# Moving the load of x from ScalarE's queue into SyncE's, between the two parts of wq

## The chip, the cores and the metric

The kernel runs on one core of a Trainium2 chip. The metric is the device time of one execution in microseconds. TensorE (PE), VectorE (DVE), ScalarE (ACT) and GpSimd (POOL) compute; here SyncE (SP) only issues DMA transfers, and ACT issues one.

## The reference, cut to what matters

One decode step of a transformer block for four sequences (B = 4): layer norm, attention over the last 4096 positions of a key and value cache, an output projection with a residual, then a second layer norm and a gated MLP with a residual.

```python
# x: [4, 1, 576]; caches: [4, 16, 16384, 128]; wq: [576, 4096]; wo: [4096, 576]
def attention(x, k_cache, v_cache, wq, wo):
    q = (x @ wq).reshape(4, 1, 32, 128)              # 32 query heads, 16 key/value heads
    k, v = k_cache[:, :, -4096:], v_cache[:, :, -4096:]   # each used by 2 query heads
    p = softmax(q . k * 128 ** -0.5)
    return (p . v).reshape(4, 1, 4096) @ wo

def mlp(x, W_gate, W_up, W_down):                    # [576, 4608] twice, [4608, 576]
    gate = x @ W_gate
    return ((gate * (gate > 0)) * (x @ W_up)) @ W_down

h  = x + attention(layernorm(x), ...)
h2 = h + mlp(layernorm(h), ...)
```

All tensors are bfloat16. About 160 MB are read in one execution, 134 MB of them the window of the two caches; x itself is 4.5 KB.

## The kernel before

The program of each engine is written out by hand, in a function of its own: `prog_sync`, `prog_act`, `prog_dve`, `prog_pool`, `prog_pe`. A small class `Sched` records a name for every operation and turns each name in a list of dependencies into a wait on a semaphore, ahead of the operation. So an engine works strictly in the order of its function, and an operation that waits holds up all behind it on that engine.

**Transfers.** SP works through one list, `transfers`, in order (`prog_sync`, L265). An entry has a name, a semaphore, what must be free before, and the DMA. The buffer `pool` holds four slots of 4 MB. `add` works out from the overlaps of offsets which consumer must be done before a slot is written again. The order is:

- wq4: rows 512 to 575 of wq, 512 KB, as 128 pieces of 4 KB (L234)
- wq0: rows 0 to 511, 4 MB, four consecutive rows for each partition (L236)
- K and V by turns, 32 transfers of 4 MB, each four heads of one sequence (L238 to L242)
- wo, W_gate, W_up, W_down (L243 to L256), and at last the store of the output (L268)

The first four entries (wq4, wq0 and the first two K) wait for nothing. The first V needs the place of wq0, so it waits for the end of the projection of q (QMM).

**x.** The only transfer that SP doesn't issue is x: it is the first line of `prog_act` (L303) and goes to `x_bf`, four partitions of 1152 bytes. It has two readers: the first layer norm, and the residual late in the kernel (L443).

**What follows x.** DVE takes the moments of x first (`moments`, L374 and L376), then builds constants from an identity matrix that POOL makes: sel, par, mask, mask8 (L384 to L390). Then it takes the reciprocal and writes `xn_bf` (`rows_norm`, L379 and L380). ACT, after x's DMA, waits for the moments, takes the root (L304), and then builds dup and col (L306, L308). PE turns `xn_bf` (L476), and multiplies it first with wq4 and then with wq0 (the loop over c = 4, 0, 1, 2, 3 in `prog_pe`). ACT copies the queries out (L320), and DVE turns them after its first transpose of a K tile (L402, L428).

**The main loop.** For each of the 16 K transfers DVE transposes four quarters (L402), PE multiplies them with the queries, DVE, POOL and ACT make the softmax, and PE multiplies with V one step later. The last stages are the output projection, the second norm and the MLP, whose W_down comes in six pieces that get smaller.

Of the kernel before, what the change touches and what calls it, by code (L numbers as in the profile page):

```python
# [102 lines left out]
def bass_sequential_preLN__sliding_block_cached__glu_gated_reglu__decode_kernel(  # L103
# [12 lines left out]
    with ExitStack() as es:  # L116
        cnt = [0]

        def sb(name, shape, dt):
            return es.enter_context(nc.sbuf_tensor(name, shape, dt))  # L120
# [10 lines left out]
        x_bf = sb("x_bf", [B, D], BF16)  # L131
# [64 lines left out]
        S = Sched()  # L196
# [3 lines left out]
        transfers = []  # L200
        at = {}

        def add(name, key, off, n, consumer, make):

            free = []
            for u in list(users):
                if u[0] < off + n and off < u[1]:
                    if u[2] not in free:
                        free.append(u[2])
                    if off <= u[0] and u[1] <= off + n:  # L210
                        users.remove(u)
            users.append((off, off + n, consumer))
            at[name] = off
            transfers.append((name, key, free, lambda e: make(e, pool[:, off:off + n])))
# [12 lines left out]
        def add_V(i):  # L227
# [5 lines left out]

        add(("wq", 4), "wq4", 2 * QUAD + 4 * HQ, HQ // 2, "QMM",  # L234
            lambda e, o: e.dma_start(out=o, in_=A_wq[512:576, :].rearrange("r (u n) -> (r u) n", u=2)))
        add(("wq", 0), "wq0", 2 * QUAD, 4 * HQ, "QMM",  # L236
            lambda e, o: e.dma_start(out=o, in_=A_wq[0:512, :].rearrange("(p u) n -> p (u n)", u=4)))
        for m in range(NQUAD + VLEAD):  # L238
# [14 lines left out]
        for k, (f0, f1) in enumerate(WD):  # L253
            transfers.append((("wd", k), f"wd{k}", ["ATTN"],
                              lambda e, f0=f0, f1=f1: e.dma_start(
                                  out=pool[:, f0 * D:f1 * D], in_=B_W_down.rearrange("(p j) n -> p (j n)", j=JJ)[:, f0 * D:f1 * D])))  # L256
# [4 lines left out]
        def land(name):  # L261
            return ("L",) + (name if isinstance(name, tuple) else (name,))
# [37 lines left out]

        def prog_act(S):
            a = "scalar"
            S.dma(a, lambda e: e.dma_start(out=x_bf[:, :], in_=A_x.rearrange("b s d -> (b s) d")), "x", name=land("x"))  # L303
            S.op(a, lambda e: e.activation(out=st1[:, 14:15], in_=st1[:, 13:14], func=ACT.Sqrt, bias=eps_c[0:B, 0:1], scale=1.0),  # L304
                 deps=["D_VAR", "EPS"], name="A_STD")
            S.op(a, lambda e: e.copy(out=dup[:, :].rearrange("p (r u) -> p r u", u=2),  # L306
                                     in_=bass.AP(tensor=ident_b, offset=0, ap=[[128, 64], [1, 64], [0, 2]])), deps=["IDB"], name="DUP")
            S.op(a, lambda e: e.copy(out=col[:, :].rearrange("p (a s) -> p a s", s=NS),  # L308
                                     in_=bass.AP(tensor=ident_b, offset=0, ap=[[128, NS], [0, 128], [1, NS]])), name="COL")
# [3 lines left out]
                                           in_=bass.AP(tensor=ident_b, offset=0, ap=[[128, NS], [0, 16], [1, NS], [0, 2]]),  # L313
# [5 lines left out]
            for k in range(2):  # L319
                S.op(a, lambda e, k=k: e.copy(out=q_bf[:, k, :].rearrange("p (x e k) -> p x e k", e=2, k=32),  # L320
                                              in_=pb[QB[k]].rearrange("p (x k e) -> p x e k", e=2, k=32)), deps=["QMM"], name=f"QBF{k}")
            S.op(a, lambda e: e.copy(out=qrep[:, :, :].rearrange("p x (g y) -> p x g y", g=4),  # L322
                                     in_=sc.ap().rearrange("p (g r) -> p g r", g=4)[:, :, 0:128].rearrange("p g (x y) -> p x g y", x=4)),
# [17 lines left out]
            for i in range(NQUAD):  # L341
# [3 lines left out]
                if i >= 2:  # L345
                    deps.append(("TRP", i - 2))
                S.op(a, lambda e, i=i: e.activation(  # L347
                    out=Pb[:, (i % 2) * 1024:(i % 2 + 1) * 1024], in_=sc[:, (i % 2) * 1024:(i % 2 + 1) * 1024], func=ACT.Exp,
                    scale=SCALE, bias=bias[:, i % 2:i % 2 + 1], accum_out=rs1[:, i:i + 1]),
                    deps=deps, name=("EXP", i))  # L350
                if i + 2 < NQUAD:
                    qzero(i + 2)
            S.op(a, lambda e: e.copy(out=bass.AP(tensor=spread, offset=0, ap=[[16 * H, H], [4 * H + 1, 4], [4, H]]),
                                     in_=bass.AP(tensor=ident_b, offset=0, ap=[[128, H], [0, 4], [1, H]])),
# [102 lines left out]
        def prog_pe(S):  # L457
# [127 lines left out]
            for k, (f0, f1) in enumerate(WD):  # L585
                deps = [land(("wd", k))]
                for f in range(f0, f1):
                    if f % (JJ // 2) == 0:
                        deps = deps + [("HHT", f // (JJ // 2))]
                    for u in range(2):  # L590
# [3 lines left out]
                        deps = []  # L594

        progs = [("gpsimd", prog_pool), ("sync", prog_sync), ("scalar", prog_act), ("vector", prog_dve), ("tensor", prog_pe)]
        S.begin(False)
        for _, p in progs:
# [32 lines left out]
```

## Time and profile before

| | |
|---|---|
| median of 3 runs | 377.9 us (377.59 to 378.06) |
| profiled execution | 378.37 us, its span 377.0 us |
| busy share of the span | PE 77%, DVE 59%, ACT 14%, POOL 3% |
| read from memory | 159.58 MB, 423 GB/s over the span |
| DMA queue 1 (issued by SP) | 6488 packets, 159.59 MB |
| DMA queue 10 (issued by ACT) | 8 packets, 4.5 KB of data |
| DMA queues 8 and 14 (loads of instructions) | 11 packets, 0.15 MB |

The span is from the first to the last instruction of the profiled execution. An engine's busy share is an average over all stages. A line of the timeline has the start and the duration in microseconds, the engine (SPq and ACTq are the sequencers that issue DMAs), the line of the kernel, the operation with output and input, and in brackets how long the engine had been idle before and what ended that. DMA transfers are split over up to 16 DMA engines; each has its own ring for each queue. The trace also keeps a record of each packet (queue, start, duration, size) and of each landing on a semaphore, without the number of the DMA engine.

### The profile page before, as it was taken

How to read it: one execution, taken by the hardware profiler on the slowest of the kernel's cores; microseconds unless marked ns; L12 is line 12 of the kernel's file. 1: busy time of each engine (PE TensorE's matmuls, PEld its weight loads, DVE VectorE, ACT ScalarE, POOL GpSimd, SP SyncE). 2: the span in 40 equal slices, each digit the busy share in tenths (PEclk: the TensorE clock that was granted, in tenths of full speed). 3: DMA queues.
4: the chain of work that ended last, by engine and by line, in shares of the span. 5: the costliest groups of instructions: out<-in, count | busy, mean ns of one | idle time of the engine just before them, and what ended most of it. 6: DMA issues, size and time to landing. Idle time of an engine off the chain costs nothing.

```text
span 377.0 us, 2565 instructions
## 1 busy us (share of the span) xinstructions
PE 291.9 (77%) x1384; PEld 67.9 (18%) x740; DVE 222.5 (59%) x169; ACT 53.1 (14%) x138; POOL 12.1 (3%) x34
## 2 busy tenths in 40 slices
PE   1408299969996999499939996799689967977675
PEld 0001012212221222022202221122112211222213
DVE  3037577696859494859476856775676658221230
ACT  3003402010220012001200220021002010101020
POOL 6000000000000000000000000000000000000000
PEclk9999879998998799989998998999869995996989
DMA  8999999999999999999999999999999999999995
GB/s 334 431 445 441 403 438 440 441 418 424 437 441 428 414 441 436 435 410 441 441 426 421 435 445 428 431 422 441 431 435 415 441 435 428 447 428 416 418 417 245
DMA packets 6507, 159.74 MB, mean 424 GB/s; under 512 B 729, under 2 KB 865, under 8 KB 1633
## 3 DMA queue, kind: packets, MB, share of 16 engines
q1 hardware_dynamic: 6488, 159.59, 98.7%
q8 instruction: 8, 0.13, 0.1%
q14 instruction: 3, 0.02, 0.0%
q10 hardware_dynamic: 8, 0.00, 0.0%
HBM read 159.58 MB, written 0.00 MB: 423 GB/s over the span
## 4 chain that ended last, share of the span: by engine, by line
DMA 53%; DVE 28%; PE 15%; ACT 2%; issue 1%; SPq 1%; POOL 0%; DVEq 0%
DMA pool<-in_A_k_cache_dram 48%; DVE kT L402 19%; PE sc L464 5%; PE sc L466 5%; DMA pool<-in_B_W_down_dram 5%; DVE acc L421 4%; DVE own_sb L418 2%; PE val L464 2%; PE val L466 2%; DVE probT L415 1%; DVE rmx L405 1%; ACT P L347 1%; DVE o_bf L440 0%; ACT L347 0%; ACT qz L336 0%
## 5 line engine op out<-in xcount | busy, mean ns | idle before, releaser
L402 DVE STREAM_TRANSPOSE kT<-pool 128x2048 f32<-128x2048 f32 x64 | 142.9, 2279 | 34.9 <-DMA pool<-in_A_k_cache_dram 33.9
L464 PE MATMUL sc<-kT,qz 128*128 128x512 bf16 x240 | 104.4, 435 | 28.7 <-DVE kT L402 28.7
L466 PE MATMUL sc<-kT,qz 128*128 128x512 bf16 x256 | 110.4, 431 | 18.3 <-DVE kT L402 16.2
L464 PE MATMUL val<-pool,probT 128*64 128x512 bf16 (+2 forms) x328 | 102.4, 360 | 4.6 <-DMA pool<-in_B_W_down_dram 4.6
L466 PE MATMUL val<-pool,probT 128*64 128x512 bf16 x256 | 96.2, 379 | 0.0
L464 PEld LDWEIGHTS sc<-kT,qz 128*128 128x128 bf16 x256 | 26.9, 105 | 154.8 <-issue 76.3
L464 PEld LDWEIGHTS val<-pool,probT 128*64 128x64 bf16 (+1 forms) x328 | 31.4, 104 | 88.0 <-issue 78.1
L405 DVE TENSOR_REDUCE rmx<-sc 128x1 f32<-128x1024 f32 x16 | 19.6, 1225 | 42.4 <-PE sc L466 42.4
L342 ACT ACTIVATE pmax<-mask,rmx 128x8 f32<-128x8 f32 x16 | 4.8, 301 | 241.3 <-DVE rmx L405 241.3
L415 DVE STREAM_TRANSPOSE probT<-P 128x1024 bf16<-128x1024 bf16 x16 | 19.9, 1245 | 20.7 <-ACT P L347 20.7
L347 ACT ACTIVATE P<-sc,bias 128x1024 bf16<-128x1024 f32 x16 | 17.8, 1113 | 13.3 <-DVE bias L410 13.3
L336 ACT COPY qz<-qrep 32x128 bf16<-32x128 bf16 x64 | 18.8, 294 | 0.6
L294 POOL PARTITION_ALL_REDUCE bcm<-pmax x16 | 5.9, 367 | 312.8 <-ACT pmax L342 312.8
L421 DVE TENSOR_REDUCE acc<-own_sb 128x128 f32<-128x1024 f32 x8 | 15.2, 1895 | 0.3
L418 DVE TENSOR_TENSOR own_sb<-val,mask 128x1024 f32<-128x1024 f32 x8 | 9.5, 1193 | 8.3 <-PE val L466 8.3
L464 PE MATMUL sc<-pool,oX 128*4 128x288 bf16 x32 | 10.2, 345 | 0.4 <-ACT oX L356 0.4
L408 DVE SCALAR_TENSOR_TENSOR t<-bcm,mask 128x8 f32<-128x8 f32 x16 | 2.7, 167 | 13.3 <-POOL bcm L294 13.3
L466 PE MATMUL sc<-pool,oX 128*4 128x288 bf16 x32 | 10.2, 343 | 0.0
L464 PE MATMUL sc<-qT,sel 32*128 32x128 bf16 x4 | 0.3, 284 | 9.8 <-DVE qT L428 9.8
L443 DVE TENSOR_TENSOR h_row<-sc,x_bf 4x576 f32<-4x576 f32 x1 | 0.7, 745 | 11.9 <-PE sc L466 11.9
L464 PE MATMUL sc<-col,foe 4*128 4x512 bf16 x16 | 6.4, 399 | 0.7 <-ACT qrep L322 0.7
L464 PE MATMUL val<-pool,xnT 128*32 128x512 bf16 x16 | 2.6, 628 | 5.0 <-DMA pool<-in_A_wq_dram 5.0
(98 smaller groups left out, 74.4 us busy)
## 6 DMA issues: line engine op xcount, KB each, us to landing
pool<-in_A_k_cache_dram SPq DMA_DIRECT2D x16, 4096.0 KB, 26.9
pool<-in_A_v_cache_dram SPq DMA_DIRECT2D x16, 4096.0 KB, 26.8
pool<-in_A_wo_dram SPq DMA_DIRECT2D x1, 4608.0 KB, 18.3
pool<-in_B_W_gate_dram SPq DMA_DIRECT2D x1, 4608.0 KB, 17.8
pool<-in_B_W_up_dram SPq DMA_DIRECT2D x1, 4608.0 KB, 24.0
pool<-in_A_wq_dram SPq DMA_DIRECT2D x1, 4096.0 KB, 13.6
pool<-in_B_W_down_dram SPq DMA_DIRECT2D x1, 2016.0 KB, 13.7
pool<-in_B_W_down_dram SPq DMA_DIRECT2D x1, 1296.0 KB, 16.4
```

Of the source, the lines that this page charges most:

```text
L294: S.op(g, lambda e, i=i: e.partition_all_reduce(bcm[:, i % 2, :], pmax[:, i % 2, :], 128, bass_isa.ReduceOp.max), deps=deps, name=("PAR", i))
L336: S.op(a, lambda e, src=src, dst=dst: e.copy(out=dst, in_=src), deps=deps, name=("QZ", i) if g == 3 else None, signal=g == 3)
L342: S.op(a, lambda e, i=i: e.activation(out=pmax[:, i % 2, :], in_=mask[:, 1, :], func=ACT.Identity, bias=rmx[:, i % 2:i % 2 + 1], scale=1.0 ...
L347: S.op(a, lambda e, i=i: e.activation(out=Pb[:, (i % 2) * 1024:(i % 2 + 1) * 1024], in_=sc[:, (i % 2) * 1024:(i % 2 + 1) * 1024], func=ACT ...
L402: S.op(v, lambda e: e.transpose(out=dst, in_=src), deps=deps, name=("TR", f))
L405: S.op(v, lambda e: e.tensor_reduce(out=rmx[:, i % 2:i % 2 + 1], in_=sc[:, (i % 2) * 1024:(i % 2 + 1) * 1024], axis=AX.X, op=ALU.max), dep ...
L408: S.op(v, lambda e: e.scalar_tensor_tensor(out=t8[:, :], in0=bcm[:, i % 2, :], scalar=-SCALE, in1=mask[:, 0, :], op0=ALU.mult, op1=ALU.mul ...
L415: S.op(v, lambda e: e.transpose(out=pT[i % NPT], in_=Pb[:, (i % 2) * 1024:(i % 2 + 1) * 1024]), deps=[("EXP", i)] + ([("PV", i - NPT)] if ...
L418: S.op(v, lambda e: e.tensor_tensor(out=own_sb[:, :].rearrange("p (x d) -> p x d", d=DH), in0=val[:, :].rearrange("p (x d) -> p x d", d=DH ...
L421: S.op(v, lambda e: e.tensor_reduce(out=acc[:, w % 2, :], in_=own_sb[:, :].rearrange("p (x d) -> p d x", d=DH), axis=AX.X, op=ALU.add), de ...
L464: return e.matmul(o, lhsT=l, rhs=r, start=start, stop=stop, skip_group_check=skip)
L466: return e.add_instruction(mybir.InstMatmult(name=nc.get_next_instruction_name(), start_tensor_calc=start, stop_tensor_calc=stop, bass_ski ...
```

## The change

x becomes an entry of SP's list, after wq4 and before wq0, with the same DMA and the same semaphore, and no wait. The line in ACT's program goes. Both readers still wait for the name of x's landing.

```diff
         add(("wq", 4), "wq4", 2 * QUAD + 4 * HQ, HQ // 2, "QMM",
             lambda e, o: e.dma_start(out=o, in_=A_wq[512:576, :].rearrange("r (u n) -> (r u) n", u=2)))
+        transfers.append((("x",), "x", [], lambda e: e.dma_start(out=x_bf[:, :], in_=A_x.rearrange("b s d -> (b s) d"))))
         add(("wq", 0), "wq0", 2 * QUAD, 4 * HQ, "QMM",
             lambda e, o: e.dma_start(out=o, in_=A_wq[0:512, :].rearrange("(p u) n -> p (u n)", u=4)))
...
         def prog_act(S):
             a = "scalar"
-            S.dma(a, lambda e: e.dma_start(out=x_bf[:, :], in_=A_x.rearrange("b s d -> (b s) d")), "x", name=land("x"))
             S.op(a, lambda e: e.activation(out=st1[:, 14:15], in_=st1[:, 13:14], func=ACT.Sqrt, bias=eps_c[0:B, 0:1], scale=1.0),
                  deps=["D_VAR", "EPS"], name="A_STD")
```

## The prediction

> **What bounds the kernel now.** I read the page first: the slices, the queues and the chain.
>
> ```profile
> span 377.0 us, 2565 instructions
> ...
> DMA  8999999999999999999999999999999999999995
> ...
> q1 hardware_dynamic: 6488, 159.59, 98.7%
> ...
> q10 hardware_dynamic: 8, 0.00, 0.0%
> ...
> DMA 53%; DVE 28%; PE 15%; ACT 2%; issue 1%; SPq 1%; POOL 0%; DVEq 0%
> ```
>
> The DMA row is full in every slice but the first and the last. Queue 1 (SP's) holds 98.7% of the engines' time; queue 10 is ACT's, whose only transfer is x: 8 packets, four rows and four semaphore writes. The chain of waits names DVE and PE often, but they wait for K tiles, and SP issues each K or V about 27 us before it lands while one passes in 9.7: the queue always holds two more. So the time is: start of SP's stream, plus the stream, plus what follows the last piece of W_down. The packet records of the trace agree: each of the 16 engines takes one 32 KB packet after another, 1.21 us each, with a gap only where an instruction load cuts in.
>
> Then the timeline of the first 28 us, where the edit lies.
>
> ```profile
> 0.72 0.55 ACTq L303 DMA_DIRECT2D x_bf<-in_A_x_dram  x1
> ...
> 0.72 0.41 SPq L235 DMA_DIRECT2D pool<-in_A_wq_dram  x1
> ...
> 1.18 0.41 SPq L237 DMA_DIRECT2D pool<-in_A_wq_dram  x1
> ...
> 1.64 1.32 SPq L225 DMA_DIRECT2D pool<-in_A_k_cache_dram  x2
> 2.16 0.81 DVE L374 BATCH_NORM_STATS2 st<-x_bf 4x6 f32<-4x288 bf16 x2 [2.16 <-DMA x_bf<-in_A_x_dram]
> ...
> 5.02 1.01 DVE L384 TENSOR_REDUCE sel<-ident_b 128x128 bf16<-128x512 bf16 x1 [1.81 <-POOL ident_b L278]
> ...
> 6.79 0.42 DVE L380 TENSOR_SCALAR xn_bf<-x_bf,st 4x576 bf16<-4x576 bf16 x1
> ...
> 14.81 0.62 PE L464 MATMUL val<-pool,xnT 128*32 128x512 bf16 x4 [5.04 <-DMA pool<-in_A_wq_dram]
> ...
> 18.48 0.54 SPq L230 DMA_DIRECT2D pool<-in_A_v_cache_dram  x1
> ...
> 24.69 2.31 DVE L402 STREAM_TRANSPOSE kT<-pool 128x2048 f32<-128x2048 f32 x1 [17.48 <-DMA pool<-in_A_k_cache_dram]
> ```
>
> x has two kinds of room. DVE has its moments long before it can build sel: it idles 1.81 us for the identity. And PE, done with the odd rows of wq (wq4) at 9.77, idles 5.04 us (9.77 is 14.81 less these) until the rest (wq0) lands. Nothing in this stage limits but the stream itself.
>
> **The change, part by part.** Durations are the profiled execution's: 378.37 us, its span 377.0 and 1.37 around it; it lies 0.47 above the median of 377.9, so I add my sum to the median.
>
> *SP's queue.* x's issue comes ahead of wq0's, K0's and K1's. No row has that issue on SP. ACT's issue of the same transfer took 0.55; SP's store of the output, also four rows of 1152 bytes, took 0.35:
>
> ```profile
> 375.71 0.35 SPq L268 DMA_DIRECT2D out_dram<-out_sb  x1
> ```
>
> I take 0.40, near that row (same queue, same four rows), and keep 0.35 and 0.55. With the 0.06 between issues, wq0 is issued 0.41 to 0.61 later, at 1.59 to 1.79 instead of 1.18. The cover is wq4 in the rings: its first packets started 1.03 (first engine) to 1.36 us (last) after its issue, so wq0's packets stand ready at 2.62 to 3.15, while the engines end wq4 between 3.26 and 3.66. Even the last engine to be supplied against the first to run dry leaves 0.11 us: no gap, 0.00. With that cover gone the end would come 0.41 to 0.61 later. K0 and K1 have more: their first packets are wanted at 13.2 and 22.9. V0, the next issue, waits for the projection's end at 18.48 in either case.
>
> *The rings.* x's packets took 0.05 to 0.12 us on four engines, and will do so there again, behind wq4 instead of ahead of it: 0.00. What a ring adds between two transfers is 6 ns: wq4's semaphore write at 3.262, wq0's first packet at 3.268, though wq4 landed from 3.60 on; so the engines do not wait for a landing before the next transfer. Without a second queue beside it wq4 may start up to 0.10 us sooner (x's first packet at 1.65, wq4's at 1.75): between -0.10 and 0; I take 0, because the first packets of wq4 took up to 0.83 us against 0.16 later, on more engines than x has rows: it is the start itself that is slow there.
>
> *x's landing.* Before, 1.42 us from issue to landing, at 2.14. After, it is issued at 1.18: at the earliest it lands at 2.60; at the latest behind all of wq4, 4.06 plus a packet of 0.12, say 4.2. I take 4.1, as rings keep their order. DVE's moments then run to 5.15 (0.81, 0.20 and gaps), and sel, par, mask, mask8, the reciprocal and xn, queued behind them, move by 0.15. ACT's root, the first in its queue, moves from 3.24 to 5.2; dup and col behind it start at 5.5 instead of 5.02, and PE wants dup only at 7.94. PE's five turns and the eight matmuls of wq4 follow 0.15 later, ending at 9.92. The 5.04 us of waiting for wq0 become 4.89: on the path 0.00. That cover ends only if x lands after about 9; and then the queries, ready at 19.55, have 7.4 us more before DVE reads them at 26.93.
>
> *ACT's queue.* Its issue of 0.55 goes. The table load behind it may start before 1.36; ACT then waits for x: 0.00.
>
> Sum: 0 (bounds -0.10 and 0 with the issue hidden, +0.61 with its cover gone), so 377.9 us.
>
> The Trainium skill has a rule against this change: "DMA: Bandwidth & Descriptors", section "Issuing engines are not separate DMA queues", says that transfers of all issuing engines run interleaved on the same 16 DMA engines and that a second issuing engine saves only sequencer time. By that the move gains nothing and gives back one issue, which would be a sum above zero instead of zero if it showed. The trace agrees on the shared engines (x on ring 10 and wq4 on ring 1 start within 0.1 us of each other); the rival below called the issue shown is what the rule would make of the time.
>
> **The rivals.** About 0.2% (0.76 us) is what a measurement of this kernel can tell from no change.
>
> *The issue shown.* If wq0's descriptors take longer after a four-row transfer than after nothing, the rings run dry at 3.3 to 3.7 and every later packet is late by that: 0.41 to 0.61, 378.4 us. It decides from an issue delay of 0.72 on (3.26 less 1.18 and 1.36); it passes 0.2% only from 1.5 us. Against it: three issues on SP in a row stand 0.46 apart.
>
> *The four slow packets gone (faster).* The packet records show one oddity: four packets of wq0, started at 11.99 to 12.12 on four engines, took 1.97 to 2.34 us instead of 1.21, with no other packet beside them. These engines stay late to the end, and one of them, hit again by an 8 KB instruction load at 100.7, is the last in each later landing: the final piece of W_down lands from 372.46 to 374.83, the next-to-last engine at 374.25. Were this a trace of the second queue (x too used four engines), it would go, and the end would come 0.58 sooner, with the earlier start 0.68: 377.2 us. Against it: it comes 10 us after x, and by the order of first packets these are not the engines that started beside x's packets.
>
> *An instruction load on the slowest engine (slower).* Queue 8 moves eight loads of 16 KB. Each holds up one engine's ring by about 1.0 us and stretches its next packet by 0.5. The landings show that each hit another engine (nine of sixteen end 1.5 to 1.8 us behind the first: these eight, and one of the four slow ones that an 8 KB load hit at 78.4) and that none hit the last, which is 2.38 behind. SP's program gets an instruction longer and ACT's shorter; if that moves one load to the slowest engine, every later landing is 1.5 us later: 379.4 us. It decides as soon as one of eight does so. Against it: these look like PE's instructions (2124 of 2565 on the page), and PE's program is untouched; for it: nothing in the trace shows what ties a load to an engine.
>
> That the change does not do what it says is hard to see: both readers of x wait for the name that the new transfer carries.
>
> **How the numbers follow.** No change (everything hidden): 0.58, 377.9 us, own range 377.5 to 378.3, which is the spread of the three runs with the sum's bounds. Four slow packets gone: 0.15. Instruction load: 0.15. Issue shown: 0.12. Faster by over 0.2%: half of the second (0.68 lies just inside 0.76) 0.08, and 0.05 for scatter in the first: 0.13. Slower: 0.15, a third of the last (0.04) and 0.04 of scatter: 0.23. Within 0.2%: 0.64. The range takes in the gone packets (377.2, less 0.1 of scatter) and the shown issue (378.5 at its dearest, plus 0.3); it leaves out the instruction load: 377.1 to 378.8.
>
> **What would show it.** Right: the issues in the order wq4, x, wq0 at about 0.72, 1.18 and 1.6; DVE's first wait for x near 4.1; PE's wait for wq0 near 4.9, ended at 14.8; K0's first transpose at 24.7 as before; the last landing near 374.8; queue 10 gone. A first transpose at 25.1 or later with wq0's landing moved alike means the issue shown; wrong on x would be PE's matmuls on the odd rows starting after 10 us. If the first transpose stands and the end moves, it is the lag of single DMA engines. The forecast is wrong if the median leaves 377.1 to 378.7.

## The result, and the profile after

The changed kernel is slower: 380.14 us (median of 6 runs, 379.56 to 381.0) against 378.01 for the kernel before, a ratio of 1.0059 with a 95% interval of 1.0044 to 1.0074. That is 2.13 us. A second set of 12 runs gave 379.34, ratio 1.0034 (1.0020 to 1.0048). The forecast was no change, 377.1 to 378.8 (378.7 in its last line).

The page of the profiled execution (380.75 us, span 379.4): span, queues, and the chain of waits by engine.

```profile
span 379.4 us, 2581 instructions
...
q1 hardware_dynamic: 6496, 159.59, 98.2%
...
DMA 48%; DVE 32%; PE 15%; ACT 3%; issue 1%; SPq 1%; POOL 0%; DVEq 0%
```

Queue 10 is gone, queue 1 has x's eight packets more, and its share has gone down: the same bytes, with idle time between. The timeline of the first 27 us says where.

```profile
0.72 0.39 SPq L235 DMA_DIRECT2D pool<-in_A_wq_dram  x1
...
1.17 0.36 SPq L236 DMA_DIRECT2D x_bf<-in_A_x_dram  x1
1.58 0.34 SPq L238 DMA_DIRECT2D pool<-in_A_wq_dram  x1
...
4.22 0.81 DVE L374 BATCH_NORM_STATS2 st<-x_bf 4x6 f32<-4x288 bf16 x2 [4.22 <-DMA x_bf<-in_A_x_dram]
...
6.91 0.42 DVE L380 TENSOR_SCALAR xn_bf<-x_bf,st 4x576 bf16<-4x576 bf16 x1
...
17.19 0.62 PE L464 MATMUL val<-pool,xnT 128*32 128x512 bf16 x4 [7.30 <-DMA pool<-in_A_wq_dram]
...
26.87 2.31 DVE L402 STREAM_TRANSPOSE kT<-pool 128x2048 f32<-128x2048 f32 x1 [19.55 <-DMA pool<-in_A_k_cache_dram]
```

Down to xn_bf all is as worked out. But wq0 lands at 17.15 instead of 14.77, PE waits 7.30 us for it instead of 5.04, and K0's first transpose starts at 26.87 instead of 24.69. The final piece of W_down lands at 377.22 instead of 374.83. So 2.38 us were lost before wq0 had landed, and 2.39 is what is missing at the end. In between the difference varies a little (K0's first transpose is 2.18 later), but none of it is won back by the end.

The packet records show the loss itself. In the kernel before, each of the 16 rings started its first 32 KB packet of wq0 within 0.04 us of its end of wq4, at 3.27 to 3.66. In the changed kernel eleven do so (3.45 to 3.73). The other five, which had ended wq4, or x behind it, between 3.42 and 3.53, start at 4.43, 5.02, 5.44, 5.44 and 5.49, and these packets then take 2.10 to 2.57 us instead of 1.21. Chained by their times, the records also say where x was: three of the five late rings carried no packet of x, and two of the four rings that carried one went on at once. At 5.88 to 6.30 one packet of each other ring is slow too (1.60 to 2.00).

Four theories were on the table: **A**, wq0's issue comes too late, and some rings run dry; **B**, the four-row transfer of x in SP's rings holds them up, whatever the time; **C**, taking x from ACT's queue costs by itself; and, from the prediction, that single slow packets or instruction loads moved.

### The profile page after: what moved, and what is told of

The parts are those of the page before. It is cut to its first block, busy times and chain, and to the rows that moved or that the text cites. A ratio compares the mean times of both kernels' runs of the same rounds, so it can differ in the third digit from the quotient of the medians.

```text
span 379.4 us, 2581 instructions
## 1 busy us (share of the span) xinstructions
PE 296.2 (78%) x1400; PEld 68.4 (18%) x740; DVE 222.4 (59%) x169; ACT 52.9 (14%) x138; POOL 12.1 (3%) x34
## 4 chain that ended last, share of the span: by engine, by line
DMA 48%; DVE 32%; PE 15%; ACT 3%; issue 1%; SPq 1%; POOL 0%; DVEq 0%
DMA pool<-in_A_k_cache_dram 42%; DVE kT L402 21%; PE sc L464 6%; DMA pool<-in_B_W_down_dram 6%; PE sc L466 5%; DVE acc L421 4%; DVE own_sb L418 2%; PE val L464 2%; PE val L466 2%; DVE probT L415 2%; DVE rmx L405 2%; ACT P L347 2%; ACT pmax L342 0%; POOL bcm L295 0%; DVE o_bf L440 0%
## 5 line engine op out<-in xcount | busy, mean ns | idle before, releaser
L464 PE MATMUL sc<-kT,qz 128*128 128x512 bf16 x256 | 110.3, 431 | 42.5 <-DVE kT L402 42.1
L466 PE MATMUL sc<-kT,qz 128*128 128x512 bf16 x256 | 109.6, 428 | 0.0
L464 PE MATMUL val<-pool,probT 128*64 128x512 bf16 (+2 forms) x328 | 103.9, 373 | 3.0 <-DMA pool<-in_B_W_down_dram 3.0
L464 PEld LDWEIGHTS val<-pool,probT 128*64 128x64 bf16 (+1 forms) x328 | 32.2, 107 | 87.1 <-issue 78.1
L464 PE MATMUL sc<-pool,oX 128*4 128x288 bf16 x32 | 9.0, 314 | 0.4 <-ACT oX L356 0.4
L466 PE MATMUL sc<-pool,oX 128*4 128x288 bf16 x32 | 9.0, 314 | 0.0
```

The costliest lines, as they stand in the source:

```text
L464: return e.matmul(o, lhsT=l, rhs=r, start=start, stop=stop, skip_group_check=skip)
L466: return e.add_instruction(mybir.InstMatmult(name=nc.get_next_instruction_name(), start_tensor_calc=start, stop_tensor_calc=stop, bass_ski ...
```

## The experiments

In all of them "room" is the time from the issue of wq0 to the end of wq4 on the first ring that ends it, taken from the issue row and the packet records of the one profiled execution. Each ratio is against the kernel before, run beside it on the same chip. The room is 2.08 us in the kernel before (3.26 less 1.18) and 1.79 in the changed one (3.37 less 1.58).

**The delay alone.** x stays with ACT; SP waits for a GpSimd memset ahead of wq0.

```diff
+            S.op(g, lambda e: e.memset(dly[:, :], 0.0), name="DLY")   # after P0; dly is [128, 608] bf16
...
+        transfers[-1][2].append("DLY")                                # wq0 waits for it
```

> x stays on ACT's queue. SP waits ahead of wq0 for a GpSimd memset of 608 columns, put in after the identity's, which by qz's row (0.86 ns a column) ends at about 1.42, so that wq0 is issued near 1.55 instead of 1.18, as late as in the changed kernel (1.58), with nothing in the queue between wq4 and wq0. Theory A (late issue: some rings run dry before wq0's packets are there, and a dry ring takes 1 to 2 us to start again): slower by about 2 us, wq0 lands near 17 instead of 14.8, some first packets of wq0 start at 4.4 to 5.5. Theory B (the four-row transfer in the ring holds it up): no change, wq0 lands at 14.8. Theory C (it is the going of x from the second queue that costs): no change.

Measured: 378.62 us, ratio 1.0026 (1.0012 to 1.0041), with single runs from 377.79 to 380.49. The issue fell where it was meant to:

```profile
1.53 0.33 SPq L238 DMA_DIRECT2D pool<-in_A_wq_dram  x1
```

Room 1.91. In the profile two rings stand for 0.2 to 0.4 us after they ended wq4 (they start wq0 0.03 and 0.11 us after the last ring of all has ended it), with first packets of 1.99 and 2.31 us; three others go on at once, with first packets of 1.77 to 1.88. So lateness costs with no transfer in between (B and C forbid that), though a third of what A forecast.

**A short and a long delay** (memsets of 300 and of 1200 columns).

> The delay run with a memset of 300 columns: wq0 is issued near 1.28 instead of 1.18 (before) and 1.53 (delay run). It is wanted about 2.0 us after its issue. Theory A with an edge between 1.9 and 2.08: no change, within 0.3 us. Without an edge: plus 0.2.

> As the delay run, with a memset of 1200 columns: wq0 is issued near 2.03 instead of 1.53, x on ACT's queue. Theory A (wq0's packets come about 2 us after its issue, and the rings run dry if wq4 ends before): all 16 rings run dry, for at least 0.4 us more than in the delay run; the time is 1.5 to 3 us above the kernel before. If the delay run's loss were chance, or any wait on SP cost the same, it would be 0.7 again.

Short: 377.96 us, ratio 1.0000 (0.9992 to 1.0009), no run above 378.33. Long: 379.85 us, ratio 1.0052 (1.0038 to 1.0065).

```profile
1.27 0.33 SPq L238 DMA_DIRECT2D pool<-in_A_wq_dram  x1
...
14.72 0.62 PE L467 MATMUL val<-pool,xnT 128*32 128x512 bf16 x4 [4.64 <-DMA pool<-in_A_wq_dram]
```

These are rows of the short delay: wq0 lands as before. Its room is 2.19 (wq4 ended a little later in that run), that of the long delay 1.37. There, five rings go on at once, the first 1.47 us after the issue, and eleven start wq0 0.8 to 1.6 us after the last ring has ended wq4 (all 16 were expected to run dry). The same kind of wait costs nothing or 1.8 us, according to the room.

**x ahead of wq4, and x behind wq0**, both on SP's queue with nothing on ACT's.

```diff
+        transfers.append((("x",), "x", [], ...))    # x first: ahead of the entry wq4; x third: behind the entry wq0
-            S.dma(a, ... "x", name=land("x"))
```

> x on SP's queue as the first transfer, ahead of wq4; nothing on ACT's. wq0 follows wq4 by 0.46 us as before. A: all is later by x's issue, about 0.4 us, wq0 lands near 15.2, no ring waits between wq4 and wq0. B: four rings are held between x and wq4, one of them sets the landing: 0.4 plus 1 to 2 us. C: about as the changed kernel, plus 2 us or more.

> x on SP's queue after wq0 and ahead of K0; nothing on ACT's. x lands near 14, the projection of q ends near 21 instead of 18.5, with the queries still ahead of their first use at 26.9. A: no change, as K0's packets are wanted only at 13.2. B: four rings are held between wq0 and K0, K0 lands 1 to 2 us late, and so does all else: plus 1 to 2 us. C: plus 2 us, with slow packets in wq0.

x first: 378.47 us, ratio 1.0013 (1.0005 to 1.0022), about the 0.43 by which the stream starts later. x third: 377.94 us, ratio 1.0000 (0.9991 to 1.0008).

```profile
1.15 0.42 SPq L237 DMA_DIRECT2D pool<-in_A_wq_dram  x1
1.62 0.37 SPq L238 DMA_DIRECT2D x_bf<-in_A_x_dram  x1
...
14.25 0.81 DVE L374 BATCH_NORM_STATS2 st<-x_bf 4x6 f32<-4x288 bf16 x2 [14.25 <-DMA x_bf<-in_A_x_dram]
...
23.95 2.31 DVE L402 STREAM_TRANSPOSE kT<-pool 128x2048 f32<-128x2048 f32 x1 [6.60 <-DMA pool<-in_A_k_cache_dram]
```

In these rows of x third, x reaches its reader 12 us later than before, and nothing is lost: K0's first transpose is no later than before. No ring stops for more than 0.1 us between wq4 and wq0 in x first, or behind x's packets in x third, and ACT's queue is idle in both: B falls, and so does C in the form that an idle ACT queue always costs. Room 2.16 and 2.11.

**A copy of x between wq4 and wq0**, read by nobody, with x itself left on ACT's queue.

```diff
+        transfers.append((("xcp",), "xcp", [], lambda e: e.dma_start(out=x_cp[:, :], in_=A_x.rearrange("b s d -> (b s) d"))))
```

> x stays on ACT's queue for its readers, and SP loads a second copy of x (four rows, read by nobody) between wq4 and wq0. A: plus 2 us, as in the changed kernel, since wq0 is issued at about 1.6. B: plus 2 us too. C: no change. With the delay alone this tells whether the transfer or the time of the issue counts.

Measured: 378.73 us, ratio 1.0021 (1.0009 to 1.0032), single runs 377.68 to 379.97. It costs, as A and B have it, but less than the changed kernel did.

**More cover.** The changed kernel with a longer wq4, which moves bytes that nobody needs. First wq4's rows read twice (1 MB), and the kernel before with the same.

```diff
-            lambda e, o: e.dma_start(out=o, in_=A_wq[512:576, :].rearrange("r (u n) -> (r u) n", u=2)))
+            lambda e, o: e.dma_start(out=o.rearrange("p (c n) -> p c n", c=2),
+                                     in_=bass.AP(tensor=wq4.tensor, offset=wq4.offset, ap=[[HQ // 2, 128], [0, 2], [1, HQ // 2]])))
```

> The changed kernel, with wq4's rows read twice by the one transfer (1 MB instead of 512 KB, the second copy unused), so that the rings are busy 1.2 us longer before wq0 is wanted. Theory A: no ring runs dry; the time is that of the kernel before plus 1.2 us of transfer, 379.1, that is 1.0 less than the changed kernel though it moves more. Theory B (the four-row transfer holds the rings): 380.1 plus 1.2, so 381.3.

> The kernel before (x on ACT's queue) with the same doubled wq4, as the measure for the run above: 377.9 plus 1.2 is 379.1. A: the two are equal within 0.3 us. B: this one is 2 us faster.

Changed with cover: 379.23 us, ratio 1.0032 (1.0019 to 1.0044). Before with the same: 379.41, ratio 1.0037 (1.0024 to 1.0049).

```profile
1.66 0.34 SPq L240 DMA_DIRECT2D pool<-in_A_wq_dram  x1
...
15.60 0.62 PE L466 MATMUL val<-pool,xnT 128*32 128x512 bf16 x4 [4.48 <-DMA pool<-in_A_wq_dram]
```

In this row of the changed kernel with cover, wq0 is issued later than in the changed kernel, and lands 1.6 us sooner, though 512 KB more go ahead of it. Its room is 3.14; all 16 rings start wq0 within 0.01 us, with first packets of 1.21 us. The two kernels cost 1.15 and 1.33 us, about the 1.2 estimated for the transfer. This is the run that A and B disagreed on most (379.1 against 381.3), and A is right.

Then in smaller doses: 64 KB and 192 KB more in wq4 (each of the 128 pieces starts 256 or 768 columns earlier).

> The changed kernel, with each of wq4's 128 pieces 512 bytes longer (64 KB in all, unused), so that the rings stay busy 0.15 us longer; wq0 is then wanted about 1.95 us after its issue instead of 1.79. Theory A with a sharp edge near 2 us: most of the 2.1 us goes, total plus 0.6 to 1.2 over the kernel before. Theory A without an edge (each ring late by what it lacks): 2.1 less 0.15 plus 0.15, so 2.1 as the changed kernel.

> As the run with 64 KB more, with 192 KB more (0.45 us); wq0 is wanted 2.24 us after its issue, against 2.08 in the kernel before. Theory A: no ring runs dry, the time is that before plus the 0.45 of transfer, 378.4. B or any fixed price of x on SP's queue: 380.1 or more.

64 KB more: 379.53 us, ratio 1.0036 (1.0023 to 1.0049), room 2.03. 192 KB more: 378.74, ratio 1.0020 (1.0012 to 1.0029), room 2.21; of its 0.72 us the transfer is 0.45. So the larger dose takes most of the loss away. The smaller one leaves 1.51, between the 0.6 to 1.2 expected of a sharp edge and the 2.1 expected without one. The packet records speak against a sharp edge too. With 192 KB more, the ring that ended first (wq4 at 3.78, x at 3.83) had a room of 2.2 and still stood until 4.94, while the other 15 went on at once. With 64 KB more, three rings stood for 0.2 to 0.6 us, none of them one of x's four, and their first packets took 2.46 to 2.57 us.

**The second queue.** The run with the unread copy on SP had lost 0.8, the changed kernel 2.1, at the same time of issue. Two differences were left: who reads the late x, and whether ACT's queue moves anything. So the changed kernel was given an unread copy of x on ACT's queue; and x first was given the delay.

> The changed kernel, with a copy of x that nobody reads loaded on ACT's queue beside wq4, as x was before. The readers use the copy that SP loads. Theory A with rings that start wq4 a little later when the second queue has work (wq4 ended at 3.40 with it, 3.37 without): as the run with the unused copy on SP, about plus 0.8. If it is the late x for its readers that costs the rest: plus 2.1, as the changed kernel.

> The run with x as SP's first transfer, and a wait for a GpSimd memset ahead of wq0, so that wq0 is issued 0.82 us after wq4 (0.41 in that run, 0.86 in the changed kernel), with no transfer between them and nothing on ACT's queue. That run was 0.55 above the kernel before. If ACT's transfer beside wq4 is what kept the loss of the delay run at 0.7: plus 0.5 and about 2, near 380.3. If it is the time alone: plus 0.55 and 0.7, near 379.2. If a transfer between wq4 and wq0 is needed for the full loss: near 379.2 too, or less.

With the copy: 378.70 us, ratio 1.0025 (1.0012 to 1.0037), single runs 377.86 to 380.16. x first with the delay (room 1.51): 380.53 us, ratio 1.0051 (1.0034 to 1.0068), single runs 378.27 to 381.21. The late reader costs nothing: with the copy on ACT's queue it reads the late x, and the run loses no more than the one with the unread copy on SP (378.70 and 378.73). The 380.53 is near what was expected if ACT's early transfer helps (380.3, against 379.2 for the time alone), but its room came out at 1.51 where the delay run had 1.91, so it can't tell the two apart. Whether ACT's transfer helps was then asked on one chip: the copy issued only after the first root (at 5.18 us), the changed kernel again, the copy again.

> The changed kernel, with the unread copy of x on ACT's queue again, but issued behind the first root, near 5.6 us, when all rings have either started wq0 or not. If ACT's transfer helps because it runs beside wq4 and the start of wq0: no help here, 380.1, plus 2.1. If it is enough that the program uses a second queue at all: 378.7, as with the copy at the start.

> The changed kernel once more, on the same chip as the two runs with the unread copy on ACT's queue: 380.1, 379.5 to 381.

> The changed kernel with the unread copy of x on ACT's queue at the start, once more, on the same chip: 378.7. If it is as slow as the changed kernel here, the difference between them was the chip's or chance.

Late copy: 379.62 us, 1.0035 (1.0021 to 1.0049). Changed again: 379.34, 1.0034 (1.0020 to 1.0048). Copy again: 378.59, 1.0021 (1.0004 to 1.0038). The changed kernel came out below the 379.5 to 381 expected. The order of the medians is the one of a helpful early transfer, but the intervals overlap. What these runs show beyond doubt is scatter: the changed kernel alone gave 378.16 to 380.77, while none of the runs of the kernel before beside it was above 378.53. Its profiled execution here was the fastest:

```profile
1.58 0.34 SPq L238 DMA_DIRECT2D pool<-in_A_wq_dram  x1
...
14.25 0.62 PE L464 MATMUL val<-pool,xnT 128*32 128x512 bf16 x4 [4.48 <-DMA pool<-in_A_wq_dram]
...
24.17 2.31 DVE L402 STREAM_TRANSPOSE kT<-pool 128x2048 f32<-128x2048 f32 x1 [16.96 <-DMA pool<-in_A_k_cache_dram]
```

Same program and same time of issue as in the profile above, but no ring was more than 0.03 us late, and the execution took 378.16 us, like the kernel before. Against those rows, K0's first transpose is 2.70 us earlier and the span 2.6 shorter (376.8 against 379.4). So the change does not cost 2 us each time; it takes the room away, and an execution then loses anything from nothing to about 3 us (381.0 was the slowest of all its runs).

**wq0 ahead of wq4**, x on ACT's queue, to see whether an order that can't be late beats both kernels.

> The kernel before with wq0 ahead of wq4 in SP's list (x on ACT's queue): the second transfer of the queue is then wanted some 10 us after its issue, never late. wq4 lands about where wq0 did, and PE's 16 matmul pairs on wq0 come after it; the queries end near 19, still ahead of their use at 26.9. Theory A: not slower than the kernel before; the small loss that its own slow first packets of wq0 may hold (6.1 us over 16 rings, 0.4 each) goes at most: 377.6 to 378.0.

Measured: 378.18 us, ratio 1.0005 (0.9996 to 1.0013). No gain. No version here beats the kernel before.

| run | room, us | ratio |
|---|---|---|
| before with doubled wq4 | 3.63 | 1.0037, of which 0.0032 transfer |
| changed, doubled wq4 | 3.14 | 1.0032, all of it transfer |
| changed, 192 KB more | 2.21 | 1.0020, of which 0.0012 transfer |
| short delay | 2.19 | 1.0000 |
| x first | 2.16 | 1.0013, of which 0.0011 later start |
| x third | 2.11 | 1.0000 |
| before | 2.08 | 1 |
| changed, 64 KB more | 2.03 | 1.0036, of which 0.0004 transfer |
| delay | 1.91 | 1.0026 |
| copy of x between | 1.82 | 1.0021 |
| changed, first and second set | 1.79, 1.78 | 1.0059, 1.0034 |
| changed, copy on ACT's queue, twice | 1.84, 1.77 | 1.0025, 1.0021 |
| changed, late copy | 1.76 | 1.0035 |
| x first, with delay | 1.51 | 1.0051 |
| long delay | 1.37 | 1.0052 |

By the medians, every run with a room of 2.08 us or more costs at most 0.3 us beyond its bytes and its start, and every run below costs 0.2% or more. Below, the loss does not grow evenly as the room shrinks (0.32% beyond the bytes at 2.03, 0.21% at 1.82), and the profiled executions of four runs between 1.76 and 1.84 took 377.86 to 378.32 us, no longer than the kernel before does. So the room says whether a loss is likely, not how large it will be.

## Why the prediction was wrong

*What bounds the kernel*: right. The loss at wq0 (2.38) came out at the end whole (2.39), as the stream's start plus the stream plus the tail has it.

*SP's queue*: the issue row was right (x took 0.36, forecast 0.40; wq0 at 1.58, forecast 1.59 to 1.79). The step that failed is the next one: "wq0's packets stand ready at 2.62 to 3.15", with the conclusion that "even the last engine to be supplied against the first to run dry leaves 0.11 us". I took the 1.03 to 1.36 us from issue to first packet from the queue's first transfer and used it for the second. In the first profile of the changed kernel the five late rings got theirs 2.85 to 3.91 us after the issue; in the long delay the first ring had its own after 1.47. So the time is longer for the second transfer, and far from the same on every ring, while the prediction had allowed 0.33 us between the first and the last. By the medians a room of about 2.0 to 2.1 us is what it takes. By that the kernel before had next to nothing to spare (2.08), and its profile may have held a sign: first packets of wq0 of up to 1.41 us, where with doubled wq4 they all take 1.21.

*The price*: also wrong. I priced a missed start at the delay, 0.41 to 0.61. In the first profile of the changed kernel a late ring loses 1.6 to 3.1 us (its start 0.7 to 1.8 after the last of the others, its first packet 0.9 to 1.4 longer), and the last ring sets each landing. In other runs the stand is short and the slow first packet is most of the price (64 KB more: 0.2 to 0.6 and 1.2 to 1.4).

*The rings*: right. x's packets took 0.05 us each in the first profile, and a ring is late without them too: in the profiles of the changed kernel and of its versions with 64 and 192 KB more, 3 of the 12 rings that carried x were late, and 6 of the 36 others.

*x's landing*: right. Forecast 4.1, measured 4.22 at its reader; xn_bf forecast 0.15 later, measured 0.12; no cost, even at 14.25 in x third.

*The rivals*. The issue shown is what happened, already with 0.40 us of delay instead of the 0.72 I gave, and with a larger price. The four slow packets near 12 us have nothing to do with ACT's queue: they are there with x on SP's, first or third (1.50 to 1.77 us). The instruction loads: eight in both profiles, the first of them in the changed kernel at 61.6, long after wq0 has landed late, and the shift of the last landing (2.39) is that of wq0 (2.38), so no load explains it.

*The Trainium skill*. "DMA: Bandwidth & Descriptors", section "Issuing engines are not separate DMA queues", spoke against the change and had the sign. It calls the saved sequencer time "usually small relative to the DMA itself"; here 0.41 us of it, at the start of the stream, cost 1.35 to 2.13. That x and wq4 started within 0.1 us of each other, which the prediction took as agreement on the shared engines, does not show them: the records give no engine.

Open is why the second transfer's packets come so late on some rings, why a late ring's first packet is slow as well, why both vary from one execution to the next, and whether ACT's early transfer makes a loss rarer. That a late issue is the cause is shown by the delays and by the longer wq4; what happens between the issue and the packets is in no record.

## What to carry to other kernels

In a kernel bound by one DMA stream, the second transfer's issue has to be early enough to be ready when the first one drains; a small transfer put in between takes that room, and it is free only where the queue already holds more than it drains. Take the time from issue to readiness from a transfer in the same place, not from the first one, and count a margin of a tenth of a microsecond as none. A thin margin may not show as a fixed price: it can show as scatter. When a kernel's runs scatter more than those of its neighbour, compare the profiles of two of its executions that differ: here the packets at one place told the two apart.

## What the runs showed of the hardware

- wq4's first packet started 1.00 to 1.24 us after the start of wq4's issue row, in all runs that had it ahead of wq0; in the kernel before the last of its rings followed at 1.36. The Trainium skill, "DMA: Bandwidth & Descriptors", section "Latency and other measured facts", gives about 0.6 us to the first byte. Counted from the start of the issue row, none of the transfers looked at here was so quick; x on ACT's queue took 0.93 in the kernel before, and the store of the output 0.77 in the changed one.
- The second transfer's packets started, ring by ring, from 1.47 us after its issue (long delay) to 3.91 (changed kernel, first profile) and 4.63 (x first with the delay). With a room of 2.08 us or more the median lost at most 0.3 us. With 1.8 us, the same program lost nothing in one execution and 2.4 us in another.
- A ring that ran dry at the start of the stream stood for 0.9 to 2.1 us in the first profile of the changed kernel, and its first 32 KB packet then took 2.1 to 2.6 us instead of 1.21. In the long delay, where eleven rings stood, their first packets took 1.4 to 1.6 us.
- 4.3 to 4.9 us after wq0's issue, in three of the profiles with a loss, rings that had started in time had one slow packet as well: eleven of 1.6 to 2.0 us at 5.9 to 6.3 in the changed kernel, eight of 1.7 to 2.0 at 6.0 to 6.2 with the copy between, eleven of 1.4 to 2.0 at 6.3 to 6.9 in x first with the delay. The profile with 64 KB more has the loss without them. What this is was not found.
